# Float64 weights to float32 by hand: the sign kept in an exponent bit, and the exclusive or left out

## The chip, the core and the metric

The kernel runs on one core of one Trainium2 chip. The metric is the device time of one execution in microseconds (us). TensorE is called PE here, its weight loads PEld, VectorE DVE, ScalarE ACT, GpSimd POOL and SyncE SP. Each engine takes its instructions in the order in which they were queued.

## The reference

```python
# attention: q, k, v are (8, 8, 576, 64) float32, tau = 0.02
scores = (1 / sqrt(64)) * q @ k.transpose(0, 1, 3, 2)
keep   = scores >= scores.max(-1, keepdims=True) - tau
attn   = softmax(where(keep, scores, -1e9))
x      = (attn @ v).transpose(0, 2, 1, 3).reshape(4608, 512)
# gated feed-forward: w_gate, w_val are (512, 1536), w_out is (1536, 512), all float64
g   = x @ w_gate
out = ((g / (1 + exp(-g))) * (x @ w_val)) @ w_out     # float32, (4608, 512)
```

The weights reach the device as float64. [...]

## The kernel before, in words

The program is one unrolled stream per engine. The first half of its source issues instructions in an order written out by hand; from the line with `plan = Plan()` on, a small planner (class `Plan`) orders the work of DVE, ACT, POOL and SP by costs that are written beside each job, such as `job("ACT", 0.93, ...)`. The matmuls stand in a fixed order; the planner fits the other engines' jobs around them.

**Attention.** A pair of heads is handled at a time, in tiles of 128 query rows. For one tile, PE makes the scores (L462) into two PSUM buffers of two banks each. DVE takes the row maxima (L479), ACT the exponentials (L482) and the threshold (L484), and DVE cuts what lies below the threshold and sums the rows (L487). PE turns the result (L517, L520), ACT copies it out of PSUM (L521, L528), and one or two tiles later PE multiplies it by v (L545 to L550), ACT copies that (L557), and POOL multiplies by the reciprocal of the row sums (L558). The next tile's scores need the PSUM buffer that the cut has read.

**Head of the program.** The first eight passes of the loop over `segs[:2 * NP]` do the attention of batch 0: four pairs with two tiles each, then the same four pairs with three tiles each. In the second four, the matmuls of the first gates and values of the feed-forward network are put between the attention tiles (`fill`). The conversion of the weights is spread over these tiles, about one piece per tile. A piece is 128 partitions by 768 weights, and there are 24: 16 of `w_gate` and `w_val` together, 8 of `w_out`.

**One piece.** `fetch_weights` (L306) queues its DMAs on SP, into one of seven landing places, as soon as the place is not in `used`. `split_weights` has ACT read the upper words as float32 (L322: magnitude, scaled by 2 to the -96) and the lower words as integers (L323: scaled, less 2). POOL clamps the first result to a range (L315). `shift_weights` has DVE shift it left by three bits (L342), which drops the exponent's extra bits. `join_weights` has DVE take the sign bit from the landing place and put it in by an exclusive or (L348), which frees the landing place; it is called after the maxima of the next tile. `add_lower` has POOL add the lower part as an integer (L358). The last three pieces are left to the planner (L890 to L904), with the same steps. `need` runs the steps at once where a gate's matmul would be too early.

Other work on POOL in the head is the scaling of q by 1/8 (L395). q is loaded in parts, and a scaling waits for its part's DMA. The order in POOL's queue is the order in which the source issues: in each tile the add of an earlier piece, the weighing of x (L558), the clamp of the new piece, and in some tiles a scaling of q.

**The rest.** Batches 1 to 7 run through the planner. The feed-forward products there use sums and differences of blocks of x and of the weights (two levels of a seven-product scheme), so that seven products stand for eight. Before, the factor 1/2 that belongs to the gate (a sigmoid written as a hyperbolic tangent of half the argument) is applied where ACT and DVE read the gate's products from PSUM: `activation(..., AF.Copy, scale=0.5)` and `scalar_tensor_tensor(scalar=0.5)`.

Of the kernel before, what the change touches and what calls it, by code (L numbers as in the profile page):

```python
# [12 lines left out]
U64 = mybir.dt.uint64  # L13
AF = mybir.ActivationFunctionType
# [114 lines left out]
def kernel(  # L129
# [182 lines left out]
    early_slots, clamped, unclamped, shifted, unsummed = [True], [], deque(), [], []  # L312

    def clamp(eng, x):
        eng.tensor_scalar(out=x, in0=x, scalar1=1.875 * 2.0 ** -80, scalar2=2.0 ** -111, op0=ALU.min, op1=ALU.max)  # L315

    def split_weights():
        if fetched:
            dst, place = fetched.popleft()
            lo = los[0].rearrange("p (m n) -> p m n", m=dst.shape[1])  # L320
            los.rotate(1)
            nc.scalar.activation(dst, words(place, dst, 1).bitcast(F32), AF.Abs, scale=2.0 ** -96)  # L322
            nc.scalar.activation(lo, words(place, dst, 0), AF.Identity, bias=minus2, scale=-2.0 ** -51)  # L323
            unclamped.append(dst)
            if early_slots[0]:
                clamp_split()
            split.append((dst, place, lo))
# [7 lines left out]
    def shift_weights(n=1):  # L335

        steps = [split.popleft() for _ in range(min(n, len(split)))]
        if any(up is x for up, place, lo in steps for x in unclamped):
            clamp_split()
        for up, place, lo in steps:  # L340
            ub = up.bitcast(U32)
            nc.vector.tensor_scalar(out=ub, in0=ub, scalar1=3, scalar2=None, op0=ALU.logical_shift_left)  # L342
        shifted.extend(steps)

    def join_weights():
        for up, place, lo in shifted:
            ub = up.bitcast(U32)
            nc.vector.scalar_tensor_tensor(out=ub, in0=words(place, up, 1), scalar=0x80000000, in1=ub,  # L348
                                           op0=ALU.bitwise_and, op1=ALU.bitwise_xor)
            used.discard(place)  # L350
        unsummed.extend(shifted)
        shifted.clear()
        add_lower(min(1, len(unsummed)))

    def add_lower(n):
        for up, place, lo in unsummed[:n]:
            ub = up.bitcast(U32)
            nc.gpsimd.tensor_tensor(out=ub, in0=ub, in1=lo.bitcast(U32), op=ALU.add)  # L358
            joined.append(up)
        del unsummed[:n]  # L360

    def need(n):
        if len(joined) < n:
            join_weights()
            add_lower(2)
        while len(joined) < n:
            fetch_weights(2)
            if not split:
                split_weights()
            shift_weights()  # L370
            join_weights()
            split_weights()
# [159 lines left out]
    def attend_tile(copy=lambda xa, fn: (fn(), give_back(xa))):  # L532
# [23 lines left out]
        def weigh():  # L556
            nc.scalar.copy(both, xa[:, 0:2 * n])  # L557
            nc.gpsimd.tensor_tensor(out=to, in0=both[:, 0:n], in1=both[:, n:2 * n], op=ALU.mult)  # L558
# [21 lines left out]
    def gate(j, f, gts):  # L580
        gts[f] = gate_places[0], tanh_places[0]
        gate_places.rotate(1)
        tanh_places.rotate(1)
        need(NCC * ((f + GR - 1) * P // FW + 1))
        whole, ps = yield from rows_of_products(j, f, 0, "pg")
        nc.scalar.activation(gts[f][1], ps, AF.Tanh, scale=0.5)
        nc.scalar.activation(gts[f][0], ps, AF.Copy, scale=0.5)
        give_back(whole)
        yield 1
# [126 lines left out]
    for n, seg in enumerate(segs[:2 * NP]):  # L716
# [3 lines left out]
        for x, t in enumerate(seg["tiles"]):  # L720
            go = scores(seg, t)
            next(go)
            join_weights()
# [28 lines left out]
            add_lower(1)  # L752
# [35 lines left out]
    join_weights()  # L788
# [79 lines left out]
    def rest_of_weights():  # L868
# [5 lines left out]
        for n, (dst, srcs, place, lo) in enumerate(todo):  # L874
# [9 lines left out]
            if lo is None:  # L884
                lo = los[0].rearrange("p (m n) -> p m n", m=m)
                los.rotate(1)
                before = joins[-3] if len(joins) > 2 else None

                def up_part(dst=dst, place=place):
                    nc.scalar.activation(dst, words(place, dst, 1).bitcast(F32), AF.Abs, scale=2.0 ** -96)  # L890

                def lo_part(dst=dst, place=place, lo=lo):
                    nc.scalar.activation(lo, words(place, dst, 0), AF.Identity, bias=minus2, scale=-2.0 ** -51)

                j = job("ACT", 0.93, up_part, j if srcs else landed, done.get(place), under, rank=2)
                j = job("ACT", 1.03, lo_part, j, before, rank=2)
            ub = dst.bitcast(U32)
            if not any(dst is x for x in clamped):
# [3 lines left out]
            j = job("DVE", 0.96, lambda ub=ub, dst=dst, place=place: nc.vector.scalar_tensor_tensor(  # L902
                out=ub, in0=words(place, dst, 1), scalar=0x80000000, in1=ub, op0=ALU.bitwise_and, op1=ALU.bitwise_xor), j, rank=2)
            j = job("POOL", 1.85, lambda ub=ub, lo=lo: nc.gpsimd.tensor_tensor(out=ub, in0=ub, in1=lo.bitcast(U32), op=ALU.add), j, rank=2)  # L904
            joins.append(j)
            done[place] = j
# [88 lines left out]
    class Group:  # L995
# [34 lines left out]
        def p5(self):  # L1030
            self.take_b()
            self.e = take("pe")
            m = self.mul(self.e, self.w[2], xs[0], True, *self.w_deps[2], *ready_x[self.c][1], *self.e.deps)
            self.e.bank.full = True
            s, old = turn_of(s_bufs)
            self.s = s
            self.s5 = job("ACT", 0.55, lambda: nc.scalar.activation(s.ap, self.e.rows(), AF.Copy, scale=0.5), m, *old, rank=0)
# [14 lines left out]
        def p6(self):  # L1052
# [9 lines left out]
            self.u1 = job("ACT", 0.55, lambda: nc.scalar.activation(u.ap, self.b.rows(), AF.Copy, scale=0.5), m, *self.u1_old, rank=0)  # L1062
# [17 lines left out]
        def p3(self):  # L1080
            m = self.mul(self.e, self.w[5], xs[2], False, self.s5, *self.w_deps[5], *ready_x[self.c][4])
            u = self.u1_buf
            g1 = job("DVE", 0.7, lambda: nc.vector.scalar_tensor_tensor(out=u.ap, in0=self.e.rows(), scalar=0.5, in1=u.ap, op0=ALU.mult,  # L1083
                                                                        op1=ALU.add), m, self.u1, rank=0)
# [4 lines left out]
        def p7(self):  # L1089
# [3 lines left out]
            self.u2 = job("ACT", 0.55, lambda: nc.scalar.activation(u.ap, self.b.rows(), AF.Copy, scale=0.5), m, *old, rank=0)  # L1093
# [76 lines left out]
    class LateGroup(Group):  # L1170
# [14 lines left out]
        def p5(self):  # L1185
# [5 lines left out]
            self.c5 = [job("ACT", 0.57, lambda: nc.scalar.activation(q0, self.es[0].ap(), AF.Copy, scale=0.5), m, *old, rank=0),  # L1191
                       job("ACT", 0.46, lambda: nc.scalar.activation(q1, self.es[1].ap()[:, 0:3 * P], AF.Copy, scale=0.5), m, *old, rank=0)]
# [7 lines left out]
        def p3(self):  # L1200
# [8 lines left out]
            g1 = job("DVE", 0.62, lambda: nc.vector.scalar_tensor_tensor(out=u.ap, in0=y, scalar=0.5, in1=u.ap, op0=ALU.mult, op1=ALU.add),  # L1209
# [4 lines left out]
    def plain_group(t, g, n_bufs):  # L1214
# [18 lines left out]
        tj = job("ACT", 0.6, lambda: nc.scalar.activation(n.ap, ps, AF.Tanh, scale=0.5), m, *n_old, rank=1)  # L1233
        cj = job("ACT", 0.6, lambda: nc.scalar.activation(u.ap, ps, AF.Copy, scale=0.5), m, *u_old, rank=1)
# [644 lines left out]
    def attend(seg):  # L1879
# [24 lines left out]
        for a in range(R):  # L1904
            def copy(a=a):
                nc.scalar.copy(xk[:, a], holds[a].ap()[:, lo:lo + 2 * NT * G].rearrange("p (t i q) -> p t i q", t=2, q=G))
                nc.scalar.copy(xl[:, a], holds[a].ap()[:, at_last:at_last + G])
# [263 lines left out]
```

## Time and profile before

| | |
|---|---|
| median of three runs | 1370.12 us (1367.74 to 1371.97) |
| the profiled execution | 1368.65 us |
| its span, first to last instruction | 1366.5 us |
| PE busy | 1346.2 us |
| DVE busy | 1094.1 us |
| ACT busy | 857.4 us |
| POOL busy | 710.8 us |
| mean granted clock of PE | 0.996 |

The span is what the profile covers; the time of the execution holds 2.15 us more around it. A busy time counts an instruction from its start to its end, so an engine can be busy and still be waiting inside an instruction. In lists of groups, a line gives the source line, the engine, the operation, what is written and read, how often it runs, the busy time in us, the mean length of one in ns, and the idle time of the engine just ahead of it with the instruction that ended it.

### The profile page before, as it was taken

The numbers are of one execution on the slowest core, as the hardware profiler recorded it, in microseconds if no ns is written. First come the engines' busy times: TensorE is split into PE (matmuls) and PEld (weight loads), VectorE is DVE, ScalarE is ACT, GpSimd is POOL, SyncE is SP. The second block draws the span as 40 slices with busy tenths as digits, with TensorE's granted clock in tenths as the row PEclk, the third lists the DMA queues.
The fourth block names the chain that finished last, engine by engine and source line by source line (L and its number), as shares of the span: only waits on it lengthen the run. The fifth ranks groups of instructions, "written<-read, shape, count | busy, mean of one in ns | idle before, by whom it ended". The sixth has DMA issues, their size and how long they took to land.

```text
span 1366.5 us, 39110 instructions
## 1 busy us (share of the span) xinstructions
PE 1346.2 (99%) x15598; PEld 1124.6 (82%) x15598; DVE 1094.1 (80%) x2860; ACT 857.4 (63%) x2190; POOL 710.8 (52%) x676
## 2 busy tenths in 40 slices
PE   8899999999999999999999999999999999999998
PEld 6687877777788788877888788888887788999888
DVE  6889898888887878887878777887888776797786
ACT  6788765677765777677767677677767674330330
POOL 2777698754655669434963387337843592000000
PEclk9999999999999999999999999999999999999999
DMA  7753323466426431654255514643255404424411
GB/s 173 192 197 102 72 60 114 129 177 179 114 48 167 149 81 46 183 144 113 45 170 137 152 19 138 158 139 68 74 156 145 110 27 158 149 77 142 160 54 32
DMA packets 208293, 162.31 MB, mean 119 GB/s; under 512 B 166128, under 2 KB 180464, under 8 KB 202736
## 3 DMA queue, kind: packets, MB, share of 16 engines
q1 hardware_dynamic: 203920, 158.86, 41.3%
q8 instruction: 123, 2.02, 0.6%
q10 hardware_dynamic: 4192, 0.95, 0.3%
q14 instruction: 58, 0.48, 0.1%
HBM read 138.28 MB, written 21.50 MB: 117 GB/s over the span
## 4 chain that ended last, share of the span: by engine, by line
PE 91%; DVE 4%; DMA 2%; SPq 1%; ACT 1%; issue 1%; ACTq 0%; DVEq 0%
PE pb L1012 17%; PE pa L1012 12%; PE px L1501 12%; PE sc L1761 10%; PE pe L1012 9%; PE xa L1895 9%; PE po L1294 5%; PE py L1510 5%; PE sc L1179 1%; PE sc L462 1%; PE pe L1179 1%; PE pg L1225 1%; PE pv L571 1%; PE sc L1012 1%; PE pg L571 1%
## 5 line engine op out<-in xcount | busy, mean ns | idle before, releaser
L1837 ACT ACTIVATE pall<-sc,nm 128x288 f32<-128x288 f32 x504 | 234.7, 501 | 79.1 <-DVE pall L1839 43.9
L1839 DVE SCALAR_TENSOR_TENSOR pall<-sc,th,pall 128x288 f32<-128x288 f32 x504 | 243.6, 512 | 38.5 <-ACT pall L1837 22.0
L1012 PE MATMUL pb<-xall,big 128*128 128x256 f32 x1104 | 262.0, 380 | 0.0
L1012 PEld LDWEIGHTS pb<-xall,big 128*128 128x128 f32 x1104 | 207.5, 190 | 29.6 <-issue 1.6
L1874 DVE STREAM_TRANSPOSE pall<-pall 128x576 f32<-128x576 f32 x252 | 187.9, 763 | 28.7 <-POOL pall L1869 15.2
L1872 ACT ACTIVATE pall<-pall,ri 128x288 f32<-128x288 f32 x416 | 190.5, 526 | 22.7 <-DVE ri L1860 21.9
L1012 PE MATMUL pa<-xall,big 128*128 128x256 f32 x752 | 178.9, 381 | 0.3 <-ACT sc L1019 0.3
L1012 PEld LDWEIGHTS pa<-xall,big 128*128 128x128 f32 x752 | 140.7, 190 | 20.9 <-issue 2.5
L863 POOL TENSOR_TENSOR hall<-hall,tmp 128x512 f32<-128x512 f32 x80 | 102.7, 1283 | 104.8 <-DVE hall L1071 64.5
L1761 PE MATMUL sc<-kT,qT 64*32 64x288 f32 (+1 forms) x5376 | 146.9, 345 | 1.5 <-issue 1.2
L1796 DVE TENSOR_REDUCE mx<-sc 128x2 f32<-128x576 f32 x168 | 118.3, 746 | 35.4 <-PE sc L1761 34.5
L1869 POOL TENSOR_SCALAR pall<-pall,ri 128x288 f32<-128x288 f32 x88 | 88.2, 1010 | 105.1 <-DVE ri L1860 75.9
L1761 PEld LDWEIGHTS sc<-kT,qT 64*32 64x32 f32 x5376 | 98.0, 106 | 53.3 <-issue 12.8
L1012 PE MATMUL pe<-xall,big 128*128 128x256 f32 x576 | 138.4, 383 | 0.0
L1895 PE MATMUL xa<-pall,vall 64*32 64x288 f32 x4032 | 129.4, 404 | 3.0 <-PE px L1501 2.7
L1012 PEld LDWEIGHTS pe<-xall,big 128*128 128x128 f32 x576 | 107.6, 190 | 18.7 <-issue 4.5
L1895 PEld LDWEIGHTS xa<-pall,vall 64*32 64x32 f32 x4032 | 83.4, 107 | 41.7 <-issue 5.0
L863 POOL TENSOR_TENSOR tmp<-tmp 128x512 f32<-128x512 f32 x36 | 45.9, 1276 | 83.5 <-ACT tmp L1093 83.5
L1854 ACT COPY sums<-sums 32x6 f32<-32x6 f32 x336 | 66.6, 198 | 28.0 <-DVE pall L1839 23.8
L1070 ACT ACTIVATE vall<-tmp 128x512 f32<-128x512 f32 x96 | 60.0, 627 | 34.5 <-DVE tmp L1083 27.2
L1510 PE MATMUL py<-wo,hall 128*128 128x256 f32 x336 | 74.8, 379 | 0.0
L863 POOL TENSOR_TENSOR hall<-hall 128x384 f32<-128x384 f32 (+2 forms) x67 | 67.6, 1023 | 8.9 <-PE px L1501 8.2
(268 smaller groups left out, 2493.7 us busy)
## 6 DMA issues: line engine op xcount, KB each, us to landing
big<-sums_hbm SPq DMA_DIRECT2D x42, 1024.0 KB, 5.2
big<-sums_hbm SPq DMA_DIRECT2D x48, 768.0 KB, 4.8
vall<-in_v_dram SPq DMA_DIRECT2D x112, 144.0 KB, 3.0
out_dram<-big SPq DMA_DIRECT2D x32, 256.0 KB, 2.9
qT<-in_q_dram SPq DMA_DIRECT2D x112, 72.0 KB, 4.8
kT<-in_k_dram SPq DMA_DIRECT2D x112, 72.0 KB, 3.1
wo<-in_moe_w_gate_dram SPq DMA_DIRECT2D x16, 384.0 KB, 4.2
wo<-in_moe_w_val_dram SPq DMA_DIRECT2D x16, 384.0 KB, 5.1
```

Source lines behind the costliest of these rows:

```text
L863: return lambda: nc.gpsimd.tensor_tensor(out=out, in0=a, in1=b, op=op)
L1012: nc.tensor.matmul(ps[:, i], w[:, k_, i * P:(i + 1) * P], x[:, k_, :], start=first and i == k_ == 0, stop=True, skip_group_check=True)
L1501: nc.tensor.matmul(ps, a[:, f, :], ws[n][:, f, :], start=bank_ not in begun, stop=True, skip_group_check=True)
L1510: nc.tensor.matmul(ps(), a[:, f, i * P:(i + 1) * P], operands[o][:, f, :], start=first and f == 0, stop=True, skip_group_check=True)
L1761: nc.tensor.matmul(to[g * G:(g + 1) * G], qT[hs, col:col + G], kT[hs, c * SH + lo:c * SH + hi], start=True, stop=True)
L1796: rs.append(job("DVE", 0.72 if w > 1 else 0.42, lambda h=h: nc.vector.tensor_reduce(out=mx[:, n0 + h:n1 + h + 1:max(2, n1 - n0), 0], in_=s ...
L1837: ej = job("ACT", 0.44, lambda x=x, n=n: nc.scalar.activation(ps[x], scs[x], AF.Exp, bias=nm[:, n:n + 1]), ej, rank=top, on=on[x])
L1839: masks[x] = job("DVE", 0.48, lambda x=x, n=n: nc.vector.scalar_tensor_tensor(out=ps[x], in0=scs[x], scalar=th[:, n:n + 1], in1=ps[x], op0 ...
L1869: scaled.append(job("POOL", 1.02, lambda x=x, n=n: nc.gpsimd.tensor_scalar(out=x, in0=x, scalar1=ri[:, n:n + 1], scalar2=None, op0=ALU.mul ...
L1872: scaled.append(job("ACT", 0.46, lambda x=x, n=n: nc.scalar.activation(x, x, AF.Copy, scale=ri[:, n:n + 1]), rj, rank=rank))
L1874: seg["turned"].append(job("DVE", 0.72, lambda both=both: nc.vector.transpose(out=both, in_=both), *scaled, rank=rank))
L1895: nc.tensor.matmul(holds[a].ap()[x * G:(x + 1) * G, 0:SH].rearrange("d (i q) -> d i q", q=G), vr[rs, h, j, ds], p[rs, h, :, j, :], start=( ...
```

## The change

A float64 has a sign, 11 exponent bits and 52 mantissa bits; a float32 has 8 exponent bits. In both kernels ACT's scaling brings the exponent into a range where, after the left shift by three, the bits stand where float32 has them. Before, the magnitude went that way, and the sign was put back by the exclusive or. Now the upper word keeps its sign: a leaky ReLU (`AF.Prelu`) multiplies by 2 to the -112 and, on the negative side, by 2 to the 32 more. The two sides so differ in an exponent bit, and the shift moves that bit into the place of the sign. The exclusive or goes, in the head and in the planner's three pieces.

The clamp works now on the upper 16 bits of each word as a signed integer, with a maximum and a minimum. The lower word leaves ACT as an integer with a constant bias (`AF.Copy`, bias 2 to the 23); before, it left as a float32 whose bits served as the integer, with a bias read from an SBUF tile. The weights come out with another power of two, so that the factor 1/2 of the gate leaves the gate's reads and enters where x is copied from PSUM: 0.5 for batch 0, 0.25 for the others.

The order moves with this. `join_weights` and `add_lower` are gone: POOL's add is issued directly after DVE's shift, and a landing place is free once ACT's two reads have been issued.

```diff
     def clamp(eng, x):
-        eng.tensor_scalar(out=x, in0=x, scalar1=1.875 * 2.0 ** -80, scalar2=2.0 ** -111, op0=ALU.min, op1=ALU.max)
+        top = x.bitcast(I16).rearrange("p m (n w) -> p m n w", w=2)[:, :, :, 1]
+        eng.tensor_scalar(out=top, in0=top, scalar1=float((32 << 7) - 2 ** 15), scalar2=float((31 << 7) + (7 << 4)), op0=ALU.max, op1=ALU.min)
+
+    def upper(dst, place):
+        nc.scalar.activation(dst, words(place, dst, 1).bitcast(F32), AF.Prelu, scale=2.0 ** -112, alpha=2.0 ** 32)
+
+    def lower(lo, dst, place):
+        nc.scalar.activation(lo.bitcast(I32), words(place, dst, 0), AF.Copy, bias=2.0 ** 23, scale=2.0 ** -29)
...
-            nc.scalar.activation(dst, words(place, dst, 1).bitcast(F32), AF.Abs, scale=2.0 ** -96)
-            nc.scalar.activation(lo, words(place, dst, 0), AF.Identity, bias=minus2, scale=-2.0 ** -51)
+            upper(dst, place)
+            lower(lo, dst, place)
+            used.discard(place)
...
             nc.vector.tensor_scalar(out=ub, in0=ub, scalar1=3, scalar2=None, op0=ALU.logical_shift_left)
-        shifted.extend(steps)
-
-    def join_weights():
-        for up, place, lo in shifted:
-            ub = up.bitcast(U32)
-            nc.vector.scalar_tensor_tensor(out=ub, in0=words(place, up, 1), scalar=0x80000000, in1=ub,
-                                           op0=ALU.bitwise_and, op1=ALU.bitwise_xor)
-            used.discard(place)
-        unsummed.extend(shifted)
-        shifted.clear()
-        add_lower(min(1, len(unsummed)))
-
-    def add_lower(n):
-        for up, place, lo in unsummed[:n]:
-            ub = up.bitcast(U32)
             nc.gpsimd.tensor_tensor(out=ub, in0=ub, in1=lo.bitcast(U32), op=ALU.add)
             joined.append(up)
...
             next(go)
-            join_weights()
             if not n and not x:
                 run_idle(6)
...
             clamp_split()
-            add_lower(1)
             double = t == NT and NP <= n < NP + 3
...
-            j = job("DVE", 0.96, lambda ub=ub, dst=dst, place=place: nc.vector.scalar_tensor_tensor(
-                out=ub, in0=words(place, dst, 1), scalar=0x80000000, in1=ub, op0=ALU.bitwise_and, op1=ALU.bitwise_xor), j, rank=2)
             j = job("POOL", 1.85, lambda ub=ub, lo=lo: nc.gpsimd.tensor_tensor(out=ub, in0=ub, in1=lo.bitcast(U32), op=ALU.add), j, rank=2)
             joins.append(j)
-            done[place] = j
...
-            nc.scalar.copy(both, xa[:, 0:2 * n])
+            nc.scalar.activation(both, xa[:, 0:2 * n], AF.Copy, scale=0.5)
...
-            self.s5 = job("ACT", 0.55, lambda: nc.scalar.activation(s.ap, self.e.rows(), AF.Copy, scale=0.5), m, *old, rank=0)
+            self.s5 = job("ACT", 0.55, lambda: nc.scalar.copy(s.ap, self.e.rows()), m, *old, rank=0)
...
-            g1 = job("DVE", 0.7, lambda: nc.vector.scalar_tensor_tensor(out=u.ap, in0=self.e.rows(), scalar=0.5, in1=u.ap, op0=ALU.mult,
-                                                                        op1=ALU.add), m, self.u1, rank=0)
+            g1 = job("DVE", 0.7, lambda: nc.vector.tensor_tensor(out=u.ap, in0=self.e.rows(), in1=u.ap, op=ALU.add), m, self.u1, rank=0)
```

The other edits of the diff repeat these: plain copies for scaled ones at the gate's further reads, scaled copies for plain ones at the two copies of x from PSUM.

## The prediction

> **What bounds the kernel now.** First the page: the busy line and two rows of the slices.
>
> ```profile
> span 1366.5 us, 39110 instructions
> PE 1346.2 (99%) x15598; PEld 1124.6 (82%) x15598; DVE 1094.1 (80%) x2860; ACT 857.4 (63%) x2190; POOL 710.8 (52%) x676
> PE   8899999999999999999999999999999999999998
> ```
>
> PE is idle for 1366.5 - 1346.2 = 20.3 us in all, and only the first two slices and the last are below 9. The change leaves the matmuls alone (count, shapes and order are the same in the built program), so it can win idle time of PE, or clock, and nothing else. The windows say where that is (after the length come the busy times of PE, PEld, DVE, ACT and POOL with their counts, then the granted clock, the DMA share and GB/s):
>
> ```profile
> 0.00:25.00 25.00, 20.62 (x125) 16.22 (x125) 16.23 (x44) 12.46 (x23) 5.45 (x12) 0.93 0.87 198
> 25.00:50.00 25.00, 20.91 (x170) 16.88 (x170) 21.10 (x45) 19.47 (x38) 17.12 (x16) 0.86 0.75 177
> 50.00:75.00 25.00, 23.50 (x192) 18.27 (x190) 18.98 (x41) 19.98 (x39) 17.27 (x16) 1.00 0.61 171
> 75.00:100.00 25.00, 25.00 (x196) 19.71 (x196) 22.64 (x43) 20.34 (x38) 19.46 (x17) 1.00 0.66 221
> ```
>
> Idle: 4.4, 4.1, 1.5 and 0.0 us. From 75 to 1300 us it is some 6 us in all, and the last 67 us hold 4.6 that no edit touches. In the first 50 us the granted clock also falls to 0.93 and 0.86. So the change is decided in the head, where weights are converted between attention tiles. The waits of PE up to 75 us:
>
> ```profile
> PE sc L462 <- DVE pall L487: 6.0, 4, 3.7
> PE sc L462 <- DVE qT L685: 1.5, 1, 1.5
> PE xa L548 <- ACT big L521: 1.1, 1, 1.1
> ```
>
> The longest, 3.7 us, is one stall before 39.76. The timeline, POOL, then DVE, then PE:
>
> ```profile
> 30.83 0.93 POOL L395 TENSOR_SCALAR hall<-hall,scl 128x256 f32<-128x256 f32 x1 [5.97 <-DMA hall<-in_q_dram]
> 31.72 1.81 POOL L358 TENSOR_TENSOR big<-big,extra 128x768 uint32<-128x768 uint32 x1
> 33.49 0.46 POOL L558 TENSOR_TENSOR xall<-pall 128x128 f32<-128x128 f32 x1
> 33.92 0.83 POOL L315 TENSOR_SCALAR big<-big 128x768 f32<-128x768 f32 x1
> 34.79 0.88 DVE L342 TENSOR_SCALAR big<-big 128x768 uint32<-128x768 uint32 x1 [2.43 <-POOL big L315]
> 37.92 1.05 DVE L348 SCALAR_TENSOR_TENSOR big<-wo,big 128x768 uint32<-128x768 uint32 x1
> 38.89 0.80 DVE L487 SCALAR_TENSOR_TENSOR pall<-sc,th,pall 128x576 f32<-128x576 f32 x1
> 39.76 3.24 PE L462 MATMUL sc<-pall,qT 64*128 64x288 f32 x10 [3.74 <-DVE pall L487]
> ```
>
> POOL sat 5.97 us behind a q load, then did the add, the weighing and only then the clamp that DVE's shift needed. DVE, in order, stood 2.43 us at that shift; behind it were two transposes, two maxima, the exclusive or and the cut that frees the PSUM of the next scores. The clock follows, with PE's busy time second:
>
> ```profile
> 35.50:38.96 3.46, 0.52 (x5) 0.27 (x3) 3.46 (x7) 1.60 (x4) 3.46 (x4) 1.00 0.62 127
> 38.96:42.40 3.44, 2.64 (x10) 2.18 (x10) 3.14 (x9) 2.94 (x6) 3.44 (x4) 0.50 1.02 372
> 42.40:45.80 3.40, 3.40 (x24) 2.54 (x23) 3.20 (x6) 1.91 (x4) 2.70 (x3) 0.50 0.85 132
> ```
>
> After a nearly empty stretch of 3.4 us come two at half clock.
>
> **The change, part by part.** *Exclusive or (L348, L902), 24 on DVE, removed*: 0.93 to 2.03 us each, some 29 us of DVE. It pays only where DVE sets PE. In the stall the maxima end at 37.99 and ACT's threshold at 38.32, so the cut could start at about 38.4 rather than 38.89: 0.5 us, the rest of the 1.05 being covered by ACT. In the two tiles before (cuts at 25.88 and 30.41, thresholds at 25.68 and 30.22) it is 0.2 each, and the stall swallows both.
>
> *Integer add, moved.* Each add now follows its shift at once; before, it followed the exclusive or of the next tile. In POOL's queue it is therefore moved past the q scaling of L395 (and past the weighing and clamp of the next tile). The add of 31.72 goes into the 5.97 us in which POOL stood idle: its shift ended at 21.93, the clamp ahead of it at 24.86. After the load (its DMA keeps its place on SP) come the scaling to 31.76, the weighing to 32.2, the clamp to 33.0; shift at 33.05 instead of 34.79: 1.7 us. With the 0.5: scores at 37.55 instead of 39.76, 2.2 us won. Next late is the q load, which the change does not hasten. PE, done with its transposes at 35.7 to 36.0, still idles some 1.8 us.
>
> *Clock.* 1.8 us of idle in a stretch of 3.4 leaves PE under 50% busy there. The stretch from 14.00 to 18.48 had PE busy 2.96 of 4.48 us, and the next, to 21.90, ran at 0.50; 25.30 to 28.70, busy 3.06 of 3.40, was followed by full clock. So I expect one stretch at half clock, not two: the next one would be full of work. At half clock the scores took 3.24 (2.09 at 26.75) and attend's three groups 3.06 (1.75 at 28.77), 2.46 in excess; half of it won is 1.2, both ends being 0 and 2.46. Once PE is earlier there, the second exclusive or counts: cut at 44.58, threshold ready at 44.13, 0.4.
>
> [...]
>
> *Lower word on ACT (L323), 24.* The bias becomes a constant and the output an integer. With a pointer it took 1.04 to 1.08, the constant-only L322 0.95: 0.09 less, bounds 0 and 0.12. From 42 to 58 us ACT sets the pace (its work per tile adds to 5.4 us, the tiles are 5.3 to 6.1 apart): four tiles, 0.3 us.
>
> *Upper word (L322), Abs to Prelu*: nearest row 0.95, unchanged; bounds 0.93 and 1.05. There is one ACT_TABLE_LOAD (1283 ns) before, and the built program has one too.
>
> *Clamp (L315): 22 on POOL, 2 on DVE*, from float words to the 16-bit upper halves, 4 bytes apart. No row has 16-bit data. Below: 0.42, if half the bytes were half the time. Above: 2.69, at L1869's 1010 ns for 288 elements. I take 0.83, the same operation on as many elements with constants too; the 2.69 is a rival. The two on DVE, 0.55, may go to 0.95 with nobody waiting.
>
> *SP.* A landing place is now free after the ACT reads, not after the exclusive or. Weight loads move ahead of two v loads and q remainders (four DMAs, about 2 us of issue). The first waits for ACT reads over by 25 us and is not blocked. v for pair 2 then leaves SP at 33 to 35 and is used after 38, its landing taking 3.0; the q remainders are scaled at 42.95 and later. Cost 0, or 1 to 2 us if a q remainder lands late and holds POOL as at 30.83.
>
> *Factors of two.* Scaled ACT copies of 128x512 (597 ns) become plain (580 to 590), 132 x copies go the other way, 48 SCALAR_TENSOR_TENSOR (686 to 691) become TENSOR_TENSOR (692 to 700). That is 1 to 2 us on ACT and below 1 on DVE, over 1100 us in which PE is idle 5: nothing.
>
> *The planner.* It drops 0.96 us for three pieces; the order on DVE, ACT and POOL differs from about 130 to 260 us, and PE's does not. PE's idle times there are 0.37 at 116 (behind two exclusive ors), 0.58, 0.35 and 0.16: between a win of 0.8 and a loss of 1.5. I take a win of 0.1.
>
> Sum: 2.2 + 1.2 + 0.4 + 0.3 + 0.1 = 4.2 us. From 60 us PE is full, so what is won ahead of it stays won. The profiled execution took 1368.65 (span 1366.5 and 2.15 around it), so 1364.45; it lies 1.47 below the median 1370.12, which gives 1365.9.
>
> **The rivals.** *Clock stays full.* In the forecast the scores after these wait for PE, whose transposes end at about 43.0; at full clock they wait for their cut, which ends at 42.3. Another 0.7 goes: 1365.2. For it: the phase of the stretches against the stall may split the gap. Against it: the row at 14.00.
>
> *Won and given back.* The new order from 130 us, or a q remainder behind the weight loads, costs 2 to 4 us later: 1369.0. For it: POOL is busy 25.00 of 25 us from 175 to 200, so a shuffle there has no slack. Against it: in that stretch PE waits for no POOL work.
>
> *POOL becomes the bound (slower).* If the 16-bit clamp costs 2.69, it ends at 34.9 in the stall (34.75 before), and the 1.7 and the clock are lost. Per tile POOL then has the add 1.82, weighing 0.6, clamp 2.69 and scaling 1.1, together 6.2 against 5.4: 0.8 in each of four tiles, 3.2 us. From 75 to 125 us POOL is busy 38.4 of 50; nine clamps at 1.86 more make 55, about 4 beyond. Less 0.5 for the exclusive or: 6.7 slower, 1376.8. It decides from a clamp of about 1.9 us on, where the tile's sum passes 5.4. For it: POOL's other TENSOR_SCALAR rows cost three times as much per element. Against it: those have a pointer scalar, the clamp has constants.
>
> **How the numbers follow.** Forecast 0.45, full clock 0.15, given back 0.24, POOL 0.16. A measurement here tells 0.3% from no change, 4.1 us: faster is below 1366.0, slower above 1374.2. The forecast stands on the line: 0.24 faster, 0.20 the same, 0.01 slower. Full clock gives 0.14 and 0.01; given back 0.02, 0.18 and 0.04; POOL 0.03 the same (a price between) and 0.13 slower. Together 0.40, 0.42, 0.18. The range goes from 1362.5 (every upper bound, 1.2 us more clock and 0.8 from the planner, and the spread of the runs) to 1373.5; it leaves out most of the POOL case.
>
> **What would show it.** Right: the first add on POOL before 30 us, no DVE wait for POOL of over 1.2 us at the shift, one wait of the scores of 1.5 to 2.2 us near 36, a single stretch at 0.50 after it, the clamp at 0.8 to 1.0. Wrong: a clamp over 1.9 us, POOL over 90% busy in 25 to 75, a second ACT_TABLE_LOAD, or idle time of PE over 3 us between 100 and 300.

## The result and the profile after

The changed kernel took 1390.95 us in the median of four runs (1389.94 to 1391.29), the kernel before 1369.23 on the same chip (1367.74 to 1371.97): a ratio of 1.0155, with a 95% interval of 1.0137 to 1.0173. It is 21.7 us slower, 25.1 above the forecast and 17.5 above the range's upper end. The rival "POOL becomes the bound" names the mechanism; its price, 6.7 us, is a third of what was measured. The profiled execution took 1390.64, with a span of 1388.7. The page after, its span, its busy times and PE's slices:

```profile
span 1388.7 us, 39076 instructions
PE 1354.3 (98%) x15598; PEld 1132.7 (82%) x15598; DVE 1070.5 (77%) x2836; ACT 854.6 (62%) x2190; POOL 757.4 (55%) x676
PE   8798999999999999999999999999999999999998
```

DVE has 24 instructions fewer and POOL as many as before, but POOL is busy 46.6 us longer. PE is idle 34.4 us instead of 20.3, and the second to fourth slices are 7, 9 and 8. PE's own busy time is 8.1 us longer although its matmuls are the same: up to 150 us the granted clock was 0.50 for 30.7 us, where it had been for 10.2. The windows of the head (columns as before: length, PE, PEld, DVE, ACT, POOL, clock, DMA share, GB/s):

```profile
25.00:50.00 25.00, 20.50 (x158) 16.67 (x159) 16.72 (x39) 17.79 (x35) 21.38 (x14) 0.86 0.81 201
50.00:75.00 25.00, 18.84 (x122) 13.74 (x120) 10.22 (x26) 12.55 (x26) 19.88 (x14) 0.86 0.58 149
75.00:100.00 25.00, 22.56 (x183) 18.43 (x182) 12.76 (x30) 17.32 (x34) 24.43 (x13) 0.93 0.62 208
```

From 75 to 100 us POOL is busy 24.43 of 25 where it had been 19.46, and DVE 12.76 where it had been 22.64: DVE, which the change relieves, now stands idle. What PE waits for in the first 160 us, and then what DVE waits for:

```profile
PE sc L452 <- DVE pall L477: 14.8, 8, 3.9
PE pg L561 <- POOL xall L548: 4.4, 1, 4.4
```

```profile
DVE big L352 <- POOL big L318: 26.8, 10, 5.2
```

PE's waits point at the cut (L477), as before. The second view names what is behind them: DVE stands 26.8 us at the shift (L352) until POOL has clamped (L318), and the cut is queued behind the shift. The stall that the forecast was to shorten, in the timeline, and the tile after it where PE waits for POOL itself:

```profile
30.35 0.93 POOL L385 TENSOR_SCALAR hall<-hall,scl 128x256 f32<-128x256 f32 x1 [3.03 <-DMA hall<-in_q_dram]
31.80 3.01 POOL L318 TENSOR_SCALAR big<-big 128x768 int16<-128x768 int16 x1
34.84 0.56 DVE L352 TENSOR_SCALAR big<-big 128x768 uint32<-128x768 uint32 x1 [3.45 <-POOL big L318]
58.14 3.00 POOL L318 TENSOR_SCALAR big<-big 128x768 int16<-128x768 int16 x1
64.44 0.86 POOL L548 TENSOR_TENSOR xall<-pall 128x128 f32<-128x128 f32 x2
65.36 2.93 PE L561 MATMUL pg<-xall,big 128*128 128x256 f32 x6 [4.36 <-POOL xall L548]
```

The add did move ahead of the load (POOL's wait for the q DMA fell from 5.97 to 3.03 us), but the clamp behind it takes 3.01 us instead of 0.83, so DVE's shift starts at 34.84, where it had started at 34.79. At 64.44 the weighing of x, whose input ACT had finished by 60.18, stands behind a clamp, an add and a scaling, and PE stands behind it for 4.36 us. Setting the same matmuls of the two traces against each other, the changed kernel is level with the one before at 54.5 us (times of the kernel before) and 7.3 us late by 66. Three stretches of one long and one short tile, from 78 to 127 us, add 4.0, 5.6 and 5.1. That makes 22.0; after it nothing more is lost.

### The profile page after: what moved, and what is told of

Its sections match the earlier page's. It is cut to its first block, busy times and chain, and to the rows that moved or that the text cites. A ratio compares the mean times of both kernels' runs of the same rounds, so it can differ in the third digit from the quotient of the medians.

```text
span 1388.7 us, 39076 instructions
## 1 busy us (share of the span) xinstructions
PE 1354.3 (98%) x15598; PEld 1132.7 (82%) x15598; DVE 1070.5 (77%) x2836; ACT 854.6 (62%) x2190; POOL 757.4 (55%) x676
## 4 chain that ended last, share of the span: by engine, by line
PE 88%; POOL 4%; DMA 2%; DVE 2%; issue 1%; SPq 1%; ACT 1%; ACTq 0%; DVEq 0%; POOLq 0%
PE pb L996 17%; PE pa L996 11%; PE px L1484 11%; PE sc L1744 10%; PE pe L996 9%; PE xa L1878 9%; PE po L1277 5%; PE py L1493 5%; POOL big L318 2%; PE pg L1208 2%; PE pv L1208 2%; PE sc L1162 1%; POOL big L353 1%; PE pe L1162 1%; PE sc L996 1%
## 5 line engine op out<-in xcount | busy, mean ns | idle before, releaser
L1054 ACT ACTIVATE vall<-tmp 128x512 f32<-128x512 f32 x96 | 60.0, 628 | 35.2 <-DVE tmp L1067 27.3
```

## The experiments

**The type or the rest of the change?** The first theory was that POOL is slow on 16-bit data. Three kernels separate the clamp from the rest. The changed kernel with a float clamp:

```diff
-        eng.tensor_scalar(out=top, in0=top, ..., op0=ALU.max, op1=ALU.min)
+        eng.tensor_scalar(out=x, in0=x, scalar1=1.875 * 2.0 ** -80, scalar2=2.0 ** -111, op0=ALU.min, op1=ALU.max)
```

> The changed kernel with the float clamp of the kernel before on POOL and DVE (a minimum and a maximum over the whole words; negative weights are lost by it, the times of the steps are not). All else of the change stays: Prelu, no exclusive or, adds directly behind the shifts, the new order of loads. Theory PRICE (the 16-bit clamp takes 3.0 us on POOL where the float one took 0.83, and that is the whole loss): clamps 0.83 us, no DVE wait for POOL over 1.3 us at a shift, and the forecast of the prediction comes out, about 4 us faster than before, 1365 +- 2. Theory ORDER (the loss comes from the adds, queued ahead of the q scalings, and from weight loads queued ahead of v and q): still 1380 or more, with POOL waiting at the adds and scalings.

It took 1362.88 us, a ratio of 0.9969 (0.9959 to 0.9979), with clamps of 0.84 us. The whole loss is in the clamp; whether its type or something else of it, this kernel can't tell. The other way round, the kernel before with a 16-bit clamp of the changed kernel's form:

```diff
-        eng.tensor_scalar(out=x, in0=x, scalar1=1.875 * 2.0 ** -80, scalar2=2.0 ** -111, op0=ALU.min, op1=ALU.max)
+        top = x.bitcast(I16).rearrange("p m (n w) -> p m n w", w=2)[:, :, :, 1]
+        eng.tensor_scalar(out=top, in0=top, scalar1=float(16 << 7), scalar2=float((47 << 7) + (7 << 4)), op0=ALU.max, op1=ALU.min)
```

> The kernel before with one edit: its clamp as a 16-bit maximum and minimum on the upper halves (limits 16 << 7 and (47 << 7) + (7 << 4), the same range in those bits). Exclusive or, order and loads stay. PRICE: about 20 us slower than before, 1385 to 1395, with clamps of 3.0 us and DVE waiting at the shifts; slower than the changed kernel by a few us if the exclusive or and the old order cost what the prediction said (4 us). ORDER: near 1370, for the order is the old one.

1392.55 us, ratio 1.0193 (1.0179 to 1.0207), clamps of 3.05 us: the clamp alone costs 1.9%. The third has DVE do the 16-bit clamp, just ahead of its shift:

```diff
-            clamp(nc.gpsimd, dst)
...
+            clamp(nc.vector, up)
             nc.vector.tensor_scalar(out=ub, in0=ub, scalar1=3, scalar2=None, op0=ALU.logical_shift_left)
```

> The changed kernel with the 16-bit clamp on DVE for all pieces, queued directly ahead of its shift, so a tile later than POOL's clamp was. POOL keeps only the adds. PRICE: DVE needs 0.61 us for it (its two clamps in the changed kernel took that), less than the exclusive or that went, and POOL is relieved of 0.83 to 3.0 per piece; as fast as the float clamp or faster, 1363 to 1367, and DVE's wait for POOL at the shift is gone. ORDER: the adds still follow the shifts and the loads are as in the changed kernel, so 1380 or more.

1370.88 us, ratio 1.0031 (1.002 to 1.0042), clamps of 0.64 to 0.68 us in the mean: slower than expected. With the clamps off POOL, this kernel is 0.6% slower than the one with the float clamp on POOL, which had won 0.3%: a pass on DVE ahead of the cut costs more than the change had won.

**A list of prices.** POOL's and DVE's operations alone, three times each, on 128x768 elements:

```diff
+        eng.tensor_scalar(out=a_f32[:, 0:N], in0=a_f32[:, 0:N], scalar1=LO, scalar2=HI, op0=ALU.max, op1=ALU.min)      # L35
+        eng.tensor_scalar(out=a_i16[:, 0:N], in0=a_i16[:, 0:N], scalar1=LO, scalar2=HI, op0=ALU.max, op1=ALU.min)      # L38
+        eng.tensor_scalar(out=step2(a_i16), in0=step2(a_i16), scalar1=LO, scalar2=HI, op0=ALU.max, op1=ALU.min)        # L39
+        eng.tensor_scalar(out=a_f32[:, 0:N], in0=a_f32[:, 0:N], scalar1=HI, scalar2=None, op0=ALU.min)                 # L46
...
+        dve.tensor_scalar(out=step2(a_i16), in0=step2(a_i16), scalar1=LO, scalar2=HI, op0=ALU.max, op1=ALU.min)        # L52
```

> A kernel of POOL and DVE instructions alone (no attention, no feed-forward; its output is a constant): maximum and minimum with two constants over 768 elements as float in sequence and 8 bytes apart, 32-bit integer, 16-bit integer in sequence and 4 bytes apart (also 384 of them, and with one operation), unsigned 16-bit, bfloat16, 16-bit to float and float to 16-bit, and a float multiply by a constant and by a pointer scalar; then three of them on DVE. If the price is one of the 16-bit integers: all int16 rows near 3.0 us and bfloat16 near 0.83. If it is one of the 4-byte step: the int16 row in sequence near 0.83. If it is one of the missing fast path for float in and out: int32, int16, bfloat16 and the mixed rows all near 3.0.

The groups by line, the last number but one being the mean of one in ns:

```profile
L39 POOL TENSOR_SCALAR ashort<-ashort 128x768 int16<-128x768 int16 x3 | 9.0, 2984 | 0.2
L38 POOL TENSOR_SCALAR ashort<-ashort 128x768 int16<-128x768 int16 x3 | 8.3, 2774 | 0.2
L35 POOL TENSOR_SCALAR afloat<-afloat 128x768 f32<-128x768 f32 x3 | 8.3, 2770 | 2.3 <-DVE afloat L31 2.1
L46 POOL TENSOR_SCALAR afloat<-afloat 128x768 f32<-128x768 f32 x3 | 7.0, 2320 | 0.2
```

The theory of the type falls here: floats in a row cost 2770 ns, as much as 16-bit words in a row (2774), 32-bit integers (2774), unsigned and bf16 (2767). The step of 4 bytes between 16-bit words adds 210 ns, one of 8 bytes between floats 62. But the kernel before clamps floats in 0.83. What this list has in common with the changed kernel, and not with the kernel before, is the sequence: it takes the maximum first, the kernel before takes the minimum first. The diff had exchanged the two along with the type.

**The sequence.** A second list and the kernels both ways. The list:

```diff
+        eng.tensor_scalar(out=a_f32[:, 0:N], in0=a_f32[:, 0:N], scalar1=HI, scalar2=LO, op0=ALU.min, op1=ALU.max)      # L36
+        eng.tensor_scalar(out=a_f32[:, 0:N], in0=a_f32[:, 0:N], scalar1=LO, scalar2=HI, op0=ALU.max, op1=ALU.min)      # L37
...
+        eng.tensor_scalar(out=step2(a_i16), in0=step2(a_i16), scalar1=HI, scalar2=LO, op0=ALU.min, op1=ALU.max)        # L43
```

> A second list of POOL instructions over 768 elements, nothing else of the kernel: float with the minimum first and the maximum first, each with the limits of the changed kernel and with those of the kernel before; then with the minimum first: float 8 bytes apart, int32, int16 in sequence, int16 4 bytes apart, bfloat16; then minimum and add, multiply and add. SEQUENCE: the rows with the minimum first near 0.83 whatever the type, those with the maximum first near 2.8 whatever the limits. TYPE: float rows 0.83 only with the limits of before, int16 rows 2.8 and more in either sequence.

```profile
L37 POOL TENSOR_SCALAR afloat<-afloat 128x768 f32<-128x768 f32 x3 | 8.3, 2779 | 0.2
L43 POOL TENSOR_SCALAR ashort<-ashort 128x768 int16<-128x768 int16 x3 | 3.1, 1040 | 0.2
L36 POOL TENSOR_SCALAR afloat<-afloat 128x768 f32<-128x768 f32 x3 | 2.5, 827 | 2.3 <-DVE afloat L31 2.1
```

Same engine, same data, same limits: 827 ns for minimum then maximum, 2779 for maximum then minimum. In this list 32-bit integers, 16-bit words in a row and bf16 took 827 as well with the minimum first, multiply then add took 834, and minimum then add 2783. Then the changed kernel with nothing but the sequence exchanged, which gives the same weights, as the lower limit lies below the upper one:

```diff
-        eng.tensor_scalar(out=top, in0=top, scalar1=float((32 << 7) - 2 ** 15), scalar2=float((31 << 7) + (7 << 4)), op0=ALU.max, op1=ALU.min)
+        eng.tensor_scalar(out=top, in0=top, scalar1=float((31 << 7) + (7 << 4)), scalar2=float((32 << 7) - 2 ** 15), op0=ALU.min, op1=ALU.max)
```

> The changed kernel with its 16-bit clamp's two operations in the other sequence: the minimum first and the maximum second, as the float clamp of the kernel before had them; the result is the same. In the price list a float maximum and minimum in the changed kernel's sequence took 2.77 us on POOL, as long as the 16-bit one in sequence, so the type may not be the reason. Theory SEQUENCE (POOL is fast where the minimum comes first): clamps near 0.83 us, DVE's waits at the shifts gone, time as with the float clamp, 0.9969 of before, 1362 to 1366. Theory TYPE (16-bit data is the reason after all, and the price list's float rows were slow for another one): clamps 3.0 us and 1387 to 1393.

1363.21 us, ratio 0.9956 (0.9943 to 0.9969). This version beats both kernels. And the kernel before with its float clamp turned round:

```diff
-        ... scalar1=1.875 * 2.0 ** -80, scalar2=2.0 ** -111, op0=ALU.min, op1=ALU.max)
+        ... scalar1=2.0 ** -111, scalar2=1.875 * 2.0 ** -80, op0=ALU.max, op1=ALU.min)
```

> The kernel before with its float clamp's two operations exchanged: maximum first. All else stays, the float type too. SEQUENCE: clamps 2.8 us and a time like that of the 16-bit clamp in the kernel before, 1.015 to 1.02 of it, 1385 to 1395. TYPE: no change, 1366 to 1370.

1395.11 us, ratio 1.0195 (1.0179 to 1.021): the kernel before loses as much by the sequence alone as by the whole 16-bit clamp. The clamps of the two, first of the changed kernel with the minimum first, then of the kernel before with the maximum first:

```profile
L318 POOL TENSOR_SCALAR big<-big 128x768 int16<-128x768 int16 x16 | 17.2, 1074 | 18.5 <-ACT big L321 17.8
```

```profile
L315 POOL TENSOR_SCALAR big<-big 128x768 f32<-128x768 f32 x16 | 45.1, 2824 | 10.8 <-ACT big L322 10.8
```

**From where on does the clamp decide?** The changed kernel with the minimum alone, which the first list has at 2.34 us for 16-bit words 4 bytes apart:

```diff
-        eng.tensor_scalar(out=top, in0=top, scalar1=float((32 << 7) - 2 ** 15), scalar2=float((31 << 7) + (7 << 4)), op0=ALU.max, op1=ALU.min)
+        eng.tensor_scalar(out=top, in0=top, scalar1=float((31 << 7) + (7 << 4)), scalar2=None, op0=ALU.min)
```

> The changed kernel with the minimum alone in the clamp; the maximum is left out, so very small weights are not raised. In the list of prices a single minimum on POOL took 2.32 to 2.34 us, between the 1.04 of minimum then maximum and the 3.0 of the changed kernel. Theory (POOL's sum per tile decides, from about 1.9 us on): clamps of about 2.35 us on POOL, slower than before, 1374 to 1384 us, ratio 1.004 to 1.011; POOL over 90% busy in 75 to 150 us. In proportion between the 1363.2 at 1.04 and the 1391 at 3.0 it would be 1382 at 2.35, so below that the point from which it decides shows. Rival: the loss is not POOL's time but something else that the order maximum, minimum brings: then the time is that of the minimum first, 1361 to 1366 us.

Clamps of 2.36 us and 1378.23 us, ratio 1.0085 (1.0069 to 1.01). Inside the theory's range, and between the other two; POOL was busy 24.1 to 24.3 of 25 us in each window from 75 to 150. From 1.07 to 2.36 us of clamp the ratio rises by 0.0128, from 2.36 to 3.0 by 0.0070: 0.010 and 0.011 for each microsecond. Three points can't show where a flat part ends. If the loss grows evenly above that point, these ratios put it near 1.2 us, and even at the edges of their intervals below 1.8; a flat part up to 1.9 us doesn't fit. POOL's sums, compared further down, give about 1.5.

**What carries the win?** With the minimum first, the change wins 0.4%. The forecast gave most of that to the moved add. First, in the kernel with the minimum first, the adds go back to their old places, after the next tile's maxima, without the exclusive or:

```diff
     def shift_weights():
...
+        shifted.extend(steps)
+    def join_weights():
+        unsummed.extend(shifted)
+        shifted.clear()
+        add_lower(min(1, len(unsummed)))
+    def add_lower(n):
+        for up, place, lo in unsummed[:n]:
...
             nc.gpsimd.tensor_tensor(out=ub, in0=ub, in1=lo.bitcast(U32), op=ALU.add)
```

> As the run with the minimum first, but POOL's adds are issued where the kernel before issued them: after the next tile's maxima, behind the q scaling. No exclusive or, and loads and places as in the changed kernel. If SEQUENCE holds: against the run with the minimum first this undoes the move of the add alone. The prediction gave that move 1.7 us of the stall near 36 and part of the clock's 1.2, so 1.7 to 2.9 slower than that run, 0.9982 to 0.9992 of before. If the win came from the exclusive or and the earlier weight loads, no slower than that run. If TYPE holds it is slow like the changed kernel and says nothing.

1365.13 us, ratio 0.9969 (0.9956 to 0.9981), against 0.9956 (0.9943 to 0.9969): the intervals overlap, so by the times the moved adds are worth 1.9 us or nothing. The traces tell more, in the paragraph on the stall below. Then a pass on DVE of the exclusive or's kind at its old place in addition:

```diff
     def join_weights():
+        for up, place, lo in shifted:
+            ub = up.bitcast(U32)
+            nc.vector.scalar_tensor_tensor(out=ub, in0=ub, scalar=0, in1=ub, op0=ALU.bitwise_and, op1=ALU.bitwise_xor)
```

> The kernel with the adds late and the minimum first, plus one DVE pass of the old exclusive or's kind (bitwise and, exclusive or, 128x768 uint32, constants) at the old place in each tile and in the planner's three pieces; its values change nothing. So the order of the adds and the DVE work are those of the kernel before, and what is left of the change is the form of the ACT steps, the earlier loads, the planner's order and the factors of two. Theory: the win comes from the removed pass (0.5 in the stall and some 2.7 us at the tiles of 78 to 127 us, where the earlier cuts shorten the tiles) and from the moved adds, so this gives it back: 1366 to 1370 us, ratio 0.998 to 1.001, and the matmul numbers of 127 us come at most 1.5 us earlier than before. Rival: the earlier loads and the shorter ACT steps carry the win, so that it stays at 0.995 to 0.997, 1362 to 1365 us.

1377.23 us, ratio 1.0077 (1.0065 to 1.009): more than either theory said. By 127 us PE was 2.2 us later than in the kernel before, and then came a wait of PE for ACT, 7.2 us long, that no other kernel here has. It ends at 177.40 us, where the planner sets the order; with the pass among its jobs too, it had arranged the other engines' work in another way. So the pass was put into the head alone:

> The kernel with the adds late and the minimum first, with the extra DVE pass of the exclusive or's kind in the tiles of the head alone; the planner's three pieces have no such pass, so its order from 130 us on is that of the kernel with the adds late. In the run with the pass in both, PE was 2.2 us later than before at 127 us, and lost 8 more from 155 to 182 us behind one wait of 7.2 us, in the part that the planner orders. Theory (the pass itself costs the tiles of 78 to 127 us, the planner's pieces only shuffle what follows): no such wait, and the time of before or up to 2 us more, 1366 to 1369 us, ratio 0.999 to 1.002, against 0.997 without the pass. Rival: the late loss is DVE's load, not the planner's order, and comes back here: 1374 to 1378 us. Second rival: the pass costs nothing in the head, 0.996 to 0.998.

1373.28 us, ratio 1.0044 (1.0031 to 1.0058), without the long wait. This is above what the theory gave, and by the number nearer to the first rival's 1374. But that rival's late loss isn't in the profiled execution (1370.55, the fastest of the five): PE, level with the kernel before until 78 us, is 2.1 us late at 127 us and still 2.1 at the end. The three stretches of two tiles from 78 to 127 us took 36.97 us in the kernel before and 34.26 with the adds late and no pass; with the pass:

```profile
sum 39.09, PE 36.63 PEld 29.10 DVE 37.17 ACT 28.53 POOL 30.49; mean PE 12.21 PEld 9.70 DVE 12.39 ACT 9.51 POOL 10.16
```

Against 0.9969 without it, the pass costs 0.75%, or 10 us by the ratios and 7.4 by the two profiled executions, which is more than the whole win. So what the change wins in these stretches comes from the removed pass. Its size is not that of the exclusive or: with the pass in place the kernel should take what the kernel before took, and it is 0.4% slower. The stand-in took 0.93 to 2.38 us, the exclusive or 0.93 to 2.04, so 0.75% is an upper value; what else makes up the 0.4% stays open. The version with the minimum first was run again beside the kernels of the last three questions:

> The changed kernel with the minimum ahead of the maximum, the same kernel as the run e5_min_first, beside the two others on the same chip: 1361 to 1366 us, ratio 0.994 to 0.998 to the kernel before. If the removed pass and the moved adds carry the win, it is some 4 us faster than the kernel with the pass put back; if the loads and the ACT steps carry it, the two are the same within 2 us.

1360.99 us, ratio 0.9958 (0.9946 to 0.9971): the win is the same a second time. On the same chip it is 16 us faster than the kernel with the pass in both places, where some 4 were expected; the long wait of that kernel, 7.2 us, is part of it.

## Why the prediction was wrong, point by point

**The clamp: the step that failed.** The prediction took 0.83 us, "the same operation on as many elements with constants too". It was not the same operation: the diff turned minimum, maximum into maximum, minimum, and that is worth a factor of 3.4 on floats (2779 over 827 ns). Measured: 3.01 us, above even the upper bound of 2.69. Had the term been 1.07, which is what the 16-bit words with the minimum first take, the forecast of a few microseconds won stood: 4.2 us were said, and 5.7 were measured with the minimum first, both times. That the sum came near is partly luck, since its terms did not all come true (below). The prediction put the whole uncertainty into the data's type and step. The type adds nothing: with the minimum first floats and 16-bit words in a row took 827 ns each, with the maximum first 2770 and 2774. The step of 4 bytes between 16-bit words adds 0.21 us in both sequences (1040 over 827 ns, 2984 over 2774).

**The price of POOL as the bound.** The rival's own working gave 3.2 us for four tiles up to 75 us and 4 for 75 to 125 (its 55 is 5 beyond the 50), less 0.5. Measured: 7.3 by 66 us, then 14.7. The three stretches of two tiles, the same matmuls in each kernel, summed; first before, then after, then the minimum first (the run made again), then the minimum alone:

```profile
sum 36.97, PE 36.60 PEld 29.11 DVE 33.95 ACT 28.38 POOL 28.33; mean PE 12.20 PEld 9.70 DVE 11.32 ACT 9.46 POOL 9.44
```

```profile
sum 51.70, PE 43.30 PEld 34.65 DVE 28.59 ACT 30.01 POOL 50.30; mean PE 14.43 PEld 11.55 DVE 9.53 ACT 10.00 POOL 16.77
```

```profile
sum 34.26, PE 34.26 PEld 27.28 DVE 22.11 ACT 27.30 POOL 30.05; mean PE 11.42 PEld 9.09 DVE 7.37 ACT 9.10 POOL 10.02
```

```profile
sum 42.67, PE 39.23 PEld 31.28 DVE 25.66 ACT 30.25 POOL 41.35; mean PE 13.08 PEld 10.43 DVE 8.55 ACT 10.08 POOL 13.78
```

POOL fills 50.30 of 51.70 us after, and 41.35 of 42.67 with the minimum alone: there its sum is the bound, as the rival said. With the minimum first it leaves 4.2 of 34.26 us free; shared by the nine clamps there, each could grow by some 0.5 us, to about 1.5, before POOL is full. That is an estimate from these sums, and below the 1.9 that the prediction took from tiles of 5.4 us.

Up to 66 us it is the same. From the end of the load's wait on, POOL has no more pause in the changed kernel:

```profile
30.35:68.38 38.03, 27.95 (x200) 21.79 (x200) 18.45 (x45) 21.78 (x42) 37.11 (x23) 0.85 0.82 213
```

It is busy 37.11 of 38.03 us. Five clamps in a row start 6.7 us apart (31.80 to 65.39), where the prediction set 5.4 for a tile: 6.6 us in five tiles, close to the 7.3 that PE is late by 66. The window from 50 to 75 us hides this with its 19.88 of 25, since POOL has 4.6 us of idle time in it after 70. So the sum was short: five tiles instead of four, clamps of 3.0 instead of 2.69, and adds of 2.17 to 2.23 in many places where it had 1.82. In the three stretches, by the single records, POOL's clamps rose by 17.8 us, and 3.7 more are products of L592 (L602 before) that now fall into them. Of the signs that the prediction named, the clamp over 1.9 us came; POOL over 90% busy holds for 30 to 68 us, though not for the windows of 25 us before 75. Half clock came on top: up to 150 us PE had two stretches at half clock before and five after.

**Stall: right where the clamp is short.** Forecast: scores in the stall 2.2 us earlier, a wait of some 1.8 left. In the first run with the minimum first they start at 37.71 instead of 39.76 after a wait of 1.80 instead of 3.74: 2.05 us earlier, with PE as ready as before (35.9 against 36.0). The moved add does it. With the adds late, and in the second run with the minimum first:

```profile
38.26 2.56 PE L467 MATMUL sc<-pall,qT 64*128 64x288 f32 x10 [3.60 <-DVE pall L492]
35.98 2.09 PE L452 MATMUL sc<-pall,qT 64*128 64x288 f32 x10 [1.42 <-DVE pall L477]
```

Up to the stall the matmuls of these two stand within 0.2 us of each other; behind it the second is ahead, by 2.8 us from 50 us on, and stays so through the head. DVE's shift starts at 34.13 with the adds late, after scaling, add, weighing and clamp, and at 31.85 with the add moved. Of these 2.3 us, 0.5 belong to POOL's scaling, which began that much earlier behind its load, and 1.8 to the add, where the forecast had 1.7. In the changed kernel the add before the load was done at 27.3 too; there the long clamp took the gain back.

**Clock.** The forecast was one stretch of 3.4 us at half clock behind the stall, not two. One came in the kernel with late adds, though after a gap of 3.60 us, and in the one with the clamp on DVE. The kernel with the minimum first had two, 6.83 us in a row, in its first profile and none in its second, with the same code; the windows of 25 to 50 us (PE's time second, the clock third from the end), first run and second:

```profile
25.00:50.00 25.00, 23.06 (x181) 18.57 (x178) 19.42 (x43) 20.57 (x42) 18.61 (x17) 0.86 0.86 218
```

```profile
25.00:50.00 25.00, 22.73 (x198) 18.38 (x199) 21.06 (x48) 21.43 (x43) 19.67 (x19) 1.00 0.83 218
```

So the term of 1.2 us with bounds 0 and 2.46 was a draw between the bounds, and "clock stays full" was not a rival but another outcome of the same kernel. The gap of 1.52 us near 16 us shows the same draw: half clock followed it in the kernel before and in the first run with the minimum first, and did not in the second. The stretches last 3.41 or 6.83 us in the traces, and once 10.24, from within the wait of 7.2 us on, apart from a last one that the end of its trace cuts off (2.13 us before, 2.91 after). These lengths are 3.41 us once, twice and three times. The length of the gap alone doesn't tell what follows: the gap of 1.80 us was followed by half clock, the one of 1.42 was not, and the one of 1.5 near 16 us was in two profiles, and not in the second run with the minimum first nor in the changed kernel. What else decides, the runs don't show.

**Exclusive or: right in the stall, too low after it.** The prediction gave it 0.5 and 0.4 us up to 45 us, and nothing from 60 us on, since "PE is full". The sums above say otherwise: 36.97 before and 34.26 with the minimum first, 2.7 us won where PE showed 0.4 of idle time. The place, before (DVE and PE) and with the minimum first (run again), where the second cut has ended at 73.55:

```profile
76.11 2.12 DVE L348 SCALAR_TENSOR_TENSOR big<-wo,big 128x768 uint32<-128x768 uint32 x2
78.88 0.81 DVE L487 SCALAR_TENSOR_TENSOR pall<-sc,th,pall 128x576 f32<-128x576 f32 x1
79.01 2.09 PE L462 MATMUL sc<-pall 64*128 64x288 f32 x10
```

```profile
73.99 1.36 PE L452 MATMUL sc<-pall 64*128 64x288 f32 x10
```

The ten score matmuls count as busy for 2.09 us in the one and 1.36 in the other. Before, they start at 79.01, when the second cut, which ends at 79.69, has just begun. The single records of the trace, which the row merges, have the matmuls of the first buffer start one by one from 79.01, and the first of the second buffer at 79.75, just behind that cut. From 73.99 on both buffers are free, and the group takes 1.36 us. The kernel before has groups of 1.36 us too; in the one at 72.50 the single records have the first matmuls of the two buffers start within 0.02 us of each other, side by side. At 79.01, with two cuts directly behind an exclusive or, the wait lies inside the group of matmuls, and the idle column stays at zero.

**ACT, factors of two, SP.** The lower word took 0.94 us (forecast 0.95), the leaky ReLU 0.94 (0.95), with one table load. Nothing in these runs points at the factors of two or at a late q load. **The planner** was to be worth 0.1 between a win of 0.8 and a loss of 1.5: from 127 us to the end the first run with the minimum first gave back 1.2 us, the second won 0.9. The rival "won and given back" is there in small in one run only. The prediction's 4.6 us of idle time in the last 67 us is 4.1, as the span ends at 1366.5; no term hangs on it.

**The sum.** The first run with the minimum first had half clock at the same two places and for as long as the kernel before, so the two traces can be set against each other without the clock. It is 2.05 us ahead at the stall and 1.7 at 78 us, wins 2.7 in the three stretches, and gives back 1.2. The forecast had 2.2 for the stall, 1.2 for the clock, which a draw decides, and nothing for the stretches.

## What to carry to other kernels

Two operations in one instruction can have another price when they change places, as on POOL here, with 827 and 2779 ns: look at which one comes first before taking a price from a row, and where the result allows either sequence, measure both. An engine that is busy for half of the whole time can still be full for 40 us, as POOL was in the changed kernel, busy for 55% of the span and for 37.11 of 38.03 us from 30.35 on: add up its work in the stretch where the longer instruction stands, with the times that its rows have there, and look at what stands in line behind it. Where PE shows no idle time, compare the length of the same group of matmuls between tiles or kernels, since a wait can lie inside it, as in the 2.09 us against 1.36.

## What was not expected of the hardware

On POOL, 128x768 elements took 0.83 us with minimum then maximum or multiply then add, 2.77 to 2.78 with maximum then minimum or minimum then add, and 2.13 to 2.34 with a single operation: one operation alone is slower than these two pairs. For one pair the type made no difference (827 ns with the minimum first, 2767 to 2779 with the maximum first). On DVE the same clamp, maximum first, took 0.56 us on floats. Why POOL is fast on some pairs, the runs don't show.

In the changed kernel with the float clamp DVE's shift took 0.54 us at 38.98, with POOL idle, and 2.17 where POOL's add was already running, from 32.18 for 1.83 us:

```profile
32.25 2.17 DVE L351 TENSOR_SCALAR big<-big 128x768 uint32<-128x768 uint32 x1
```

Where the shift came first, it was the other way round: in the changed kernel the shift of 34.84 took 0.56 us, and the add that started at 34.89 took 2.17 instead of 1.81.
